# Grouping the value and score products of two units of a top-k attention + SwiGLU kernel, on one core

## The chip, the cores and the metric

The kernel runs on one core of one Trainium2 chip. The metric is the device time of one execution, in microseconds (us), as the median of several runs. Engine names are those of the profile: PE is the matrix engine (TensorE) with PEld for its weight loads, DVE the vector engine, ACT the scalar engine, POOL the GpSimd engine, SP the engine that issues most DMAs.

## The reference: what is computed

Attention over 8 batches, 8 heads, 576 positions and head dimension 64, in which every query keeps only its 32 largest scores, followed by a gated feed-forward network (FFN) over the 4608 resulting rows:

```python
B, H, S, D = 8, 8, 576, 64
scores = scale * np.matmul(q, k.transpose(0, 1, 3, 2))
kth = np.partition(scores, -32, axis=-1)[..., -32:-31]
scores = np.where(scores >= kth, scores, -1e9)
attn = np.exp(scores - scores.max(-1, keepdims=True))
attn = attn / (attn.sum(-1, keepdims=True) + 1e-9)
x = np.matmul(attn, v).transpose(0, 2, 1, 3).reshape(B * S, H * D)   # 4608 x 512
g = x @ w_gate                                                      # 512 -> 1536
out = (g / (1 + np.exp(-g)) * (x @ w_val)) @ w_out                  # 1536 -> 512
```

All data are float32.

## The kernel before

The work is cut into 160 **units**. A unit is one batch, one query tile and one pair of heads; a batch has 5 query tiles x 4 pairs = 20 units. Query tiles 0 to 3 hold 128 queries (a *full* unit, both heads side by side in 1152 columns); query tile 4 holds the last 64 queries of both heads, one head above the other in 128 partitions (a *last* unit, 576 columns). With S = 576, J = 4 and JP = 512, R = 64 is what is left over: the last keys of each head.

One pass of the main loop, called iteration n here, has a stage of several units in it, in a fixed program order per engine:

```python
TURN, VALUES = 3, 4
for n in range(NU + VALUES):
    topk = select(n)                      # DVE: 4 x MAX8, 3 x MATCH_REPLACE8 per head, then e
    nxt = scores(n + 1)                   # PE products, ACT copies out of PSUM
    ahead = fetch(n + 2)                  # prep of a head pair, loads
    ...
    flush(on_act)                         # ACT: pending evacuations of the FFN
    penalize(n - 1)                       # POOL: e = e + scores
    flush(on_pool)
    run(turn(n - TURN))                   # PE transposes of e, ACT copies
    finish_unit(n - VALUES)               # values(): PE, ACT copy to xT
    next(nxt, None)                       # PE products of the scores
    early[0]()
    weigh(n - 1)                          # ACT: exp with sums
    run(nxt)                              # ACT: copies of the scores
    dve(2, beside=False)
    ...
    pieces(2)                             # PE: FFN work, as much as `credit` allows
    flush(on_act)
    dve(1); dve(1)
    run(norm)                             # ACT: scale e of unit n-2
    flush(on_pool)
    next(ahead, None); pieces(1); next(ahead, None)
    dve(1); pieces(1); dve(2); run(topk); pieces(6)
```

The stages that the change touches. PSUM tiles tagged "t" rotate over five banks (`ps_t`, bufs=5), those of the FFN over three others (`ps_f`):

```python
def prep(i):                                   # one head pair of one batch
    slab = slabs.tile([P, R + S + S], FP32, tag="kqT", name="kqT")
    for n, at in ((0, R), (None, S), (1, S + 2 * R)):
        ps = ps_t.tile([P, 512], FP32, tag="t", name="kqps")
        if n is None:                          # last keys and queries
            nc.tensor.transpose(ps[:, 0:P], kq_last[:].rearrange("p h d -> p (h d)"), ident[:])
            nc.scalar.copy(slab[:, at : at + P], ps[:, 0:P])
            nc.scalar.copy(slab[:, 0:R], ps[:, 0:R])
            yield
            continue
        for c in range(J):                     # 4 transposes, then one copy
            ...

def scores(n):
    sc = work.tile([P, 2 * S], FP32, tag="sc", name="sc", bufs=2)
    half = S // 2                              # 288
    if qt == J:
        ...                                    # 4 products of 64x64 tiles, 288 columns
    else:
        for i in range(2):
            for hh, d in enumerate(halves):    # d: partitions 0-63 or 64-127
                ps = bank()
                nc.tensor.matmul(ps[:, 0:half], slab[d, q0 : q0 + P], slab[d, k0 : k0 + half])
        yield
        for i, ps in banks:
            nc.scalar.copy(sc[:, i * half : (i + 1) * half], ps[:, 0:half])

def turn(n):                                   # e^T, 9 (full) or 5 (last) transposes
    for c0, cn in ((0, J), (J, 1)) if last else ((0, J), (J, 1), (J + 1, J)):
        ps = ps_t.tile([P, 512], FP32, tag="t", name="etps")
        ...
        nc.scalar.copy(et[0:kl, c0 : c0 + cn, :], ...)

def values(n):
    av = ps_t.tile([P, P], FP32, tag="t", name="av")
    if not last:                               # last keys of both heads, block diagonal
        nc.tensor.matmul(av[:], vl[:], et[:, J, :], start=True, stop=False)
    for c in range(J + 1 if last else J):
        for hh in range(2):                    # column tiles of 64: one head each
            nc.tensor.matmul(av[hh * R : (hh + 1) * R, 0:ql],
                             v_last[:, hh, :] if c == J else vt[:, hh, c, :], moving, ...)
    ...                                        # ACT copies av into xT

def share(n):                                  # FFN pieces that iteration n may do
    others = 0.0
    for m, cost in ((n + 1, 0.7), (n - TURN, 0.6), (n - VALUES, 0.7)):
        if m >= 0:
            others += cost * (0.5 if units[m][1] == J else 1)
    if units[n + 2][1] == 0:
        others += 0.6
    beside = 6.4 if T[1] else 7.0
    return beside * n_heads(units[n][1]) / 2 - others
```

The FFN works on blocks of 256 rows. From the second block on, its output product is done by seven `quarter(...)` products with sums on POOL; a piece of the two input products is 16 PE records, a piece of a quarter 6 records (three products; every float32 product stands in the trace as two MATMUL records). `load(i)` fetches keys and queries of a head pair with six DMAs (`k` of two heads, last keys, `q` of two heads, last queries) into a pool of two buffers. At the end of the kernel every engine's instructions are tied to program order.

Of the kernel before, what the change touches and what calls it, by code (L numbers as in the profile page):

```python
# [1 line left out]

# [13 lines left out]
P = 128  # L16
# [4 lines left out]
BLK = 256  # L21
# [6 lines left out]
def kernel(  # L28
# [34 lines left out]

    nc = tc.nc
    B, H, S, D = q.shape
    DM, DFF = w_gate.shape
# [10 lines left out]
    assert D == 64 and R == 64 and H * D == DM and DM == 512 and B * S % BLK == 0  # L79

    consts = ctx.enter_context(tc.tile_pool(name="consts", bufs=1))
    ld = ctx.enter_context(tc.tile_pool(name="ld", bufs=2))
    slabs = ctx.enter_context(tc.tile_pool(name="slabs", bufs=4))
    work = ctx.enter_context(tc.tile_pool(name="work", bufs=2))
    small = ctx.enter_context(tc.tile_pool(name="small", bufs=3))
# [4 lines left out]

    ident = consts.tile([P, P], FP32, name="ident")
    make_identity(nc, ident[:])
    NV = 4
    vlast = []
    for i in range(NV):
        vt = consts.tile([P, P], FP32, name=f"vlast{i}")
        nc.vector.memset(vt[:], 0.0)
        vlast.append(vt)
# [120 lines left out]

    pairs = [(b, hp) for b in range(B) for hp in range(NHP)]  # L220
    raw, preps = {}, {}

    def load(i):
        b, hp = pairs[i]
        h = slice(2 * hp, 2 * hp + 2)
        kq = ld.tile([P, 2, J, 2, D], FP32, tag="kq", name="kq_in")
        kq_last = ld.tile([P, 2, D], FP32, tag="kql", name="kq_last")
        for n, src in ((0, k), (1, q)):
            for hh in range(2):
                queue = nc.scalar if hh == 1 and i == 0 else nc.sync  # L230
                queue.dma_start(
                    kq[:, n, :, hh, :],
                    src[b, 2 * hp + hh, 0:JP].rearrange("(p j) d -> p j d", j=J),
                )
            nc.sync.dma_start(
                kq_last[n * R : (n + 1) * R], src[b, h, JP:S].rearrange("h p d -> p h d")
            )
        raw[i] = (kq, kq_last)
# [3 lines left out]
    def load_v(i):  # L242
        b, hp = pairs[i]
        h = slice(2 * hp, 2 * hp + 2)
        vt = slabs.tile([P, 2, J, D], FP32, tag="v", name="v")
        v_last = slabs.tile([R, 2, D], FP32, tag="vl", name="v_last")
        vl = vlast[i % NV]
        nc.sync.dma_start(
            vt[:].rearrange("p h j d -> p h (j d)"),
            v[b, h, 0:JP].rearrange("h (p j) d -> p h (j d)", j=J),  # L250
        )
        nc.sync.dma_start(v_last[:], v[b, h, JP:S].rearrange("h p d -> p h d"))
        for hh in range(2):
            o = hh * R
            nc.sync.dma_start(vl[o : o + R, o : o + R], v[b, 2 * hp + hh, JP:S])
        vs[i] = (vt, v_last, vl)

    def prep(i):

        kq, kq_last = raw.pop(i)  # L260
        slab = slabs.tile([P, R + S + S], FP32, tag="kqT", name="kqT")
        for n, at in ((0, R), (None, S), (1, S + 2 * R)):
            ps = ps_t.tile([P, 512], FP32, tag="t", name="kqps")
            if n is None:
                nc.tensor.transpose(
                    ps[:, 0:P], kq_last[:].rearrange("p h d -> p (h d)"), ident[:]
                )
# [17 lines left out]

        return 1 if qt == J else 2

    def scores(n):
        b, qt, hp = units[n]
        slab = preps[b * NHP + hp]  # L290
        sc = work.tile([P, 2 * S], FP32, tag="sc", name="sc", bufs=2)
        halves = [slice(0, D), slice(D, P)]
        half = S // 2

        def bank():
            return ps_t.tile([P, 512], FP32, tag="t", name="s")


        if qt == J:
            banks = [bank() for _ in range(2)]  # L300
            for i, ps in enumerate(banks):
                for d in halves:
                    k0 = R + i * half
                    nc.tensor.matmul(  # L304
                        ps[d, 0:half], slab[d, S + R : S + 2 * R], slab[d, k0 : k0 + half]
                    )
            yield
            for i, ps in enumerate(banks):
                nc.scalar.copy(sc[:, i * half : (i + 1) * half], ps[:, 0:half])  # L309
        else:  # L310
            q0 = S + 2 * R + qt * P
            banks = []
            for i in range(2):
                for hh, d in enumerate(halves):
                    ps = bank()
                    banks.append((i + 2 * hh, ps))
                    k0 = (1 - hh) * R + i * half
                    nc.tensor.matmul(  # L318
                        ps[:, 0:half], slab[d, q0 : q0 + P], slab[d, k0 : k0 + half]
                    )  # L320
            yield
            for i, ps in banks:
                nc.scalar.copy(sc[:, i * half : (i + 1) * half], ps[:, 0:half])  # L323
        state[n] = dict(sc=sc)

    def select(n):

# [77 lines left out]

    xT, done = {}, {}

    def values(n):

        b, qt, hp = units[n]  # L410
        vt, v_last, vl = vs[b * NHP + hp]
        et = state.pop(n)["et"]
        last = qt == J
        ql = R if last else P
        av = ps_t.tile([P, P], FP32, tag="t", name="av")
        if not last:
            nc.tensor.matmul(av[:], vl[:], et[:, J, :], start=True, stop=False)  # L417
        for c in range(J + 1 if last else J):
            kl = R if c == J else P
            for hh in range(2):  # L420
                moving = (
                    et[0:kl, c, hh * R : (hh + 1) * R]
                    if last
                    else et[:, c + hh * (J + 1), :]
                )
                nc.tensor.matmul(  # L426
                    av[hh * R : (hh + 1) * R, 0:ql],
                    v_last[:, hh, :] if c == J else vt[:, hh, c, :],
                    moving,
                    start=last and c == 0,  # L430
                    stop=c == (J if last else J - 1),
                )
        c0 = b * S + qt * P
        at = c0
        while at < c0 + ql:
            kb = at // BLK
            n_c = min((kb + 1) * BLK, c0 + ql) - at
            if kb not in xT:
                xT[kb] = ffn.tile([P, NHP, BLK], FP32, tag="xT", name="xT", bufs=3)
                done[kb] = 0  # L440
            nc.scalar.copy(
                xT[kb][:, hp, at - kb * BLK : at - kb * BLK + n_c],
                av[:, at - c0 : at - c0 + n_c],
            )
            done[kb] += n_c
            at += n_c

    def store(o, g0):

# [220 lines left out]
    def fetch(n):  # L670
# [2 lines left out]
        i = b * NHP + hp  # L673
        if qt == 0:
            yield from prep(i)
        if qt == J and i + NHP < len(pairs):
            load(i + NHP)

    def share(n):


        others = 0.0
        for m, cost in ((n + 1, 0.7), (n - TURN, 0.6), (n - VALUES, 0.7)):
            if m >= 0:
                others += cost * (0.5 if units[m][1] == J else 1)
        if units[n + 2][1] == 0:
            others += 0.6

        beside = 6.4 if T[1] else 7.0
# [7 lines left out]
    def run(steps):  # L697
        for _ in steps:
            pass

    def finish_unit(n):
        values(n)
        b, qt, hp = units[n]
        if qt == J and b + 1 < B:
            load_v((b + 1) * NHP + hp)

    load(0)
    rounding(2)
    load(1)
    run(fetch(0))  # L710
    run(scores(0))
    run(fetch(1))
    credit = [0.0]
    no = iter(())
    over = {}
    TURN, VALUES = 3, 4
    due = [2.0]
    for n in range(NU + VALUES):
# [33 lines left out]
        run(nxt)  # L752

        dve(2, beside=False)
        if 2 <= n + 2 < NHP:
            load(n + 2)
# [9 lines left out]
        flush(on_pool)  # L766
        next(ahead, None)
        pieces(1)
        next(ahead, None)
        dve(1)  # L770
        pieces(1)
        dve(2)
# [52 lines left out]
```

## Time and profile before

| | before |
|---|---|
| median of 3 runs | 1840.44 us (1838.14 to 1840.71) |
| profiled execution, span | 1835.9 us |
| DVE busy | 1618.9 us (88%) |
| ACT busy | 1202.6 us (66%) |
| POOL busy | 1013.0 us (55%) |
| MAX8 on DVE, L339 | 1152 of about 758 ns |
| PE: FFN input products, L480 | 3456 records of 382 ns |
| PE: score products of full units, L318 | 1024 records, 64-row tiles, 288 columns, 445 ns |
| PE: value products, L426 | 2560 records |
| ACT: copies of 128x288 scores, L323 | 512 of 402 ns |
| ACT: copies of 128x512, L398 | 288 of 600 ns; 128x128: 128 of 278 ns |

How to read it: "busy" counts the modelled duration of an instruction. PE records overlap (a record of 382 ns starts every 216 ns in a run of equal ones), so what a stage costs on PE is read from the starts of its records, not from the durations. A chain of waits follows the work that ended last back to the start and says which engine the time was spent on.

### The profile page before, as it was taken

The page shows a single profiled execution, that of the slowest core. Times are in us where ns is not written, and L with a number is a line of the kernel's source. Part 1 is how long each engine was busy: PE and PEld are TensorE (multiplying, and loading weights), DVE is VectorE, ACT ScalarE, POOL GpSimd, SP SyncE. Part 2 cuts the span into 40 slices and gives each one's busy share as a digit, 9 for nine tenths or more (in the row PEclk, how much of TensorE's full clock was granted, in tenths as well). Part 3 has the DMA queues.
Part 4 walks back from the last instruction along what each step waited for, and adds up shares of the span by engine and source line. Part 5 has one row for each costly group of instructions (what it writes and reads, how often), then busy time and mean ns, then how long its engine had stood idle before and what let it go on. Part 6 is the DMA issues. An engine that isn't in the chain of part 4 may idle for free.

```text
span 1835.9 us, 30517 instructions
## 1 busy us (share of the span) xinstructions
PE 1705.2 (93%) x10756; PEld 1406.3 (77%) x10756; DVE 1618.9 (88%) x3405; ACT 1202.6 (66%) x2943; POOL 1013.0 (55%) x932
## 2 busy tenths in 40 slices
PE   3448999999999989999999999999999999999998
PEld 2336758777888878887888878888788878888887
DVE  7999999999999889997999989998999989998300
ACT  5667766677666667666767676767776766675431
POOL 3556746645555545655464646564556554646444
PEclk7668999999999999999999999999999999999999
DMA  7332121000200021000300012000300011000000
GB/s 189 98 84 91 59 66 26 12 1 21 73 1 12 2 66 27 12 1 15 73 19 1 12 42 52 1 12 2 74 19 12 1 36 32 1 12 12 1 13 12
DMA packets 109145, 59.65 MB, mean 32 GB/s; under 512 B 88512, under 2 KB 96704, under 8 KB 108992
## 3 DMA queue, kind: packets, MB, share of 16 engines
q1 hardware_dynamic: 107936, 57.44, 12.1%
q8 instruction: 85, 1.39, 0.3%
q14 instruction: 68, 0.56, 0.1%
q10 hardware_dynamic: 1056, 0.26, 0.1%
HBM read 48.23 MB, written 9.44 MB: 31 GB/s over the span
## 4 chain that ended last, share of the span: by engine, by line
PE 83%; DVE 3%; POOL 2%; ACT 2%; issue 2%; POOLq 0%; ACTq 0%
PE f L480 39%; PE x_ps L566 9%; PE av L426 8%; PE etps L397 7%; PE s L318 7%; PE y_ps L566 7%; PE s L304 2%; PE av L417 1%; DVE m L339 1%; PE kqps L273 1%; DVE rest L343 1%; PE o_ps L526 1%; POOL e L361 1%; POOL p L552 0%; ACT e L370 0%
## 5 line engine op out<-in xcount | busy, mean ns | idle before, releaser
L339 DVE MAX8 m<-rest 128x8 f32<-128x576 f32 x864 | 619.3, 758 | 2.2
L343 DVE MATCH_REPLACE8 rest<-m,rest 128x576 f32<-128x576 f32 x576 | 427.1, 754 | 0.0
L361 POOL TENSOR_TENSOR e<-e,sc 128x1152 f32<-128x1152 f32 (+1 forms) x160 | 382.7, 2392 | 79.7 <-DVE e L349 61.0
L480 PE MATMUL f<-xT,wg 128*128 128x256 f32 x1728 | 401.6, 382 | 0.0
L480 PE MATMUL f<-xT,wv 128*128 128x256 f32 x1728 | 400.4, 382 | 0.0
L480 PEld LDWEIGHTS f<-xT,wg 128*128 128x128 f32 x1728 | 323.0, 190 | 62.6 <-issue 21.0
L480 PEld LDWEIGHTS f<-xT,wv 128*128 128x128 f32 x1728 | 325.3, 190 | 59.5 <-issue 16.6
L508 POOL TENSOR_TENSOR h<-h,half_g 128x512 f32<-128x512 f32 x108 | 138.1, 1279 | 295.6 <-ACT h L507 295.1
L339 DVE MAX8 m<-sc 128x8 f32<-128x576 f32 x288 | 206.4, 757 | 105.8 <-ACT sc L309 57.9
L370 ACT ACTIVATE e<-e,bias 128x576 f32<-128x576 f32 x288 | 222.1, 777 | 89.5 <-POOL e L361 89.5
L397 PE MATMUL etps<-ident,e 128*128 128x128 f32 (+1 forms) x1312 | 184.0, 285 | 96.9 <-POOL size L120 40.8
L398 ACT COPY et<-etps 128x512 f32<-128x512 f32 (+1 forms) x448 | 184.4, 484 | 124.6 <-PE etps L397 123.6
L397 PEld LDWEIGHTS etps<-ident,e 128*128 128x128 f32 (+1 forms) x1312 | 158.3, 146 | 124.3 <-POOL size L120 43.3
L513 POOL TENSOR_TENSOR h<-h,val 128x512 f32<-128x512 f32 x108 | 139.9, 1295 | 186.0 <-ACT val L512 185.8
L385 ACT ACTIVATE e<-e,tot 128x576 f32<-128x576 f32 x288 | 211.9, 789 | 7.0 <-DVE tot L382 6.7
L343 DVE MATCH_REPLACE8 rest<-m,sc 128x576 f32<-128x576 f32 x288 | 213.0, 750 | 0.0
L318 PE MATMUL s<-kqT 64*128 64x288 f32 x1024 | 171.6, 445 | 5.8 <-ACT kqT L278 3.6
L349 DVE TENSOR_SCALAR e<-sc,m 128x576 f32<-128x576 f32 x288 | 171.8, 640 | 3.4
L426 PE MATMUL av<-et,v 128*64 128x128 f32 (+1 forms) x2560 | 172.4, 280 | 0.0
L323 ACT COPY sc<-s 128x288 f32<-128x288 f32 x512 | 163.9, 402 | 1.8 <-PE s L318 1.7
L426 PEld LDWEIGHTS av<-et,v 128*64 128x64 f32 x2560 | 135.7, 144 | 22.7 <-issue 6.6
L505 ACT ACTIVATE h<-f 128x512 f32<-128x512 f32 x108 | 65.3, 605 | 130.9 <-PE f L480 130.9
(71 smaller groups left out, 2010.0 us busy)
## 6 DMA issues: line engine op xcount, KB each, us to landing
v<-in_v_dram SPq DMA_DIRECT2D x32, 256.0 KB, 3.0
kq_in<-in_k_dram SPq DMA_DIRECT2D x63, 128.0 KB, 3.0
kq_in<-in_q_dram SPq DMA_DIRECT2D x63, 128.0 KB, 3.0
w<-in_moe_w_gate_dram SPq DMA_DIRECT2D x12, 512.0 KB, 3.7
w<-in_moe_w_val_dram SPq DMA_DIRECT2D x12, 512.0 KB, 3.8
w<-in_moe_w_out_dram SPq DMA_DIRECT2D x12, 512.0 KB, 3.6
out_dram<-o SPq DMA_DIRECT2D x40, 128.0 KB, 2.4
out_dram<-o SPq DMA_DIRECT2D x16, 256.0 KB, 2.4
```

Of the source, the lines that this page charges most:

```text
L318: nc.tensor.matmul(ps[:, 0:half], slab[d, q0 : q0 + P], slab[d, k0 : k0 + half])
L339: nc.vector.max(m[:, t, 8 * r : 8 * r + 8], cur[:, hs])
L343: nc.vector.match_replace(rest[:, hs], m[:, t, 8 * r : 8 * r + 8], cur[:, hs], LOWEST)
L349: nc.vector.tensor_scalar(e[:, hs], sc[:, hs], m[:, t, TOP_K - 1 : TOP_K], FAR, ALU.is_lt, ALU.mult)
L361: nc.gpsimd.tensor_tensor(e[:, every], e[:, every], sc[:, every], ALU.add)
L370: nc.scalar.activation(e[:, hs], e[:, hs], AF.Exp, bias=bias[:, t : t + 1], scale=scale, accum_out=tot[:, t : t + 1],)
L385: nc.scalar.mul(e[:, hs], e[:, hs], tot[:, t : t + 1])
L397: nc.tensor.transpose(ps[0:kl, c * P : (c + 1) * P], e[:, k0 : k0 + kl], ident[:])
L398: nc.scalar.copy(et[0:kl, c0 : c0 + cn, :], ps[0:kl, 0 : cn * P].rearrange("p (c j) -> p c j", c=cn),)
L426: nc.tensor.matmul(av[hh * R : (hh + 1) * R, 0:ql], v_last[:, hh, :] if c == J else vt[:, hh, c, :], moving, start=last and c == 0, stop=c ...
L480: nc.tensor.matmul(ps[:, i, :], w[:, kc, m * P : (m + 1) * P], x[:, kc, :], start=(kc == 0), stop=(kc == KC - 1),)
L566: nc.tensor.matmul(ps, lhsT, T[i][m], start=m == 0, stop=m == MQ - 1)
```

## The change

It does four things. It puts the value products of two units and the score products of two units next to each other, in odd iterations only, so that PE goes through its tile shapes (128x128, 128x64 for values, 64x128 for scores) once for two units. It computes the scores against the last keys of both heads as one 128x128 product with a block-diagonal `klast`, placed beside the like product with `vlast`, and the other 512 keys of a head in one product with 512 columns instead of two with 288. It has three score buffers, so that two units can be ahead, and finds the room by giving the loads one buffer (the first loads borrow buffers of the FFN). And it moves the transposes of odd iterations behind the first FFN pieces, fetches a head pair one iteration earlier, and has new constants for how much FFN work an iteration takes.

The diff, cut to its core:

```diff
-    ld = ctx.enter_context(tc.tile_pool(name="ld", bufs=2))
+    ld = ctx.enter_context(tc.tile_pool(name="ld", bufs=1))
+    klast, vlast = [], []                       # [P, P] each, zeroed, one per head pair
 ...
 def load(i):
+        if 1 <= i < NHP:
+            kq = ffn.tile([P, 2, J, 2, D], FP32, tag="xT", name="kq_in", bufs=3)
+            kq_last = ffn.tile([P, 4, 2, D], FP32, tag="h", ...)[:, 0]
+        else:
+            kq = ld.tile(...); kq_last = ld.tile(...)[:]
 ...
 def prep(i):
-        slab = slabs.tile([P, R + S + S], FP32, tag="kqT", name="kqT")
+        slab = slabs.tile([P, JP + S], FP32, tag="kqT", name="kqT")
-                nc.scalar.copy(slab[:, at : at + P], ps[:, 0:P])
-                nc.scalar.copy(slab[:, 0:R], ps[:, 0:R])
+                for d in HALVES:
+                    nc.scalar.copy(klast[pairs[i][1]][d, d], ps[d, 0:R])
+                nc.scalar.copy(slab[:, at : at + R], ps[:, R:P])
 ...
-    def scores(n):
+    def scores(ns):
+        scs = [work.tile([P, 2 * S], FP32, tag="sc", name="sc", bufs=3) for _ in ns]
+        last = bank("last")
+        for u, (slab, hp) in enumerate(of):
+            if qt < J:
+                nc.tensor.matmul(last[:, u * P : (u + 1) * P], slab[:, queries], klast[hp][:])
+        yield
+        for u, ((slab, hp), sc) in enumerate(zip(of, scs)):
+            if qt == J:
+                mains = [bank("s")]
+                for d in HALVES:
+                    nc.tensor.matmul(mains[0][d, :], slab[d, queries], slab[d, 0:JP])
+                for d in HALVES:
+                    nc.tensor.matmul(last[d, u * P : u * P + R], slab[d, queries], klast[hp][d, d])
+            else:
+                mains = [bank("s") for _ in HALVES]
+                for d, ps in zip(HALVES, mains):
+                    nc.tensor.matmul(ps[:], slab[d, queries], slab[d, 0:JP])
+            yield
+            for hh, ps in enumerate(mains):
+                nc.scalar.copy(sc[:, hh * (S + R) : hh * (S + R) + JP], ps[:])
+            ...                                  # and the unit's part of `last`
 ...
-    def values(n):
+    def values(ns, nxt):
+        avs = [ps_t.tile([P, P], FP32, tag="t", name="av") for _ in ns]
+        if not last:
+            for n, et, av in zip(ns, ets, avs):
+                nc.tensor.matmul(av[:], vl[:], et[:, J, :], start=True, stop=False)
+        next(nxt, None)                          # the products with klast
+        for n, et, av in zip(ns, ets, avs):
+            ...                                  # as before, unit after unit
 ...
 def fetch(n):
-        if qt == J and i + NHP < len(pairs):
-            load(i + NHP)
+            if NHP <= i + 1 < len(pairs):        # right after prep(i)
+                load(i + 1)
 ...
 def share(n):
-        others = 0.0
-        for m, cost in ((n + 1, 0.7), (n - TURN, 0.6), (n - VALUES, 0.7)):
-            if m >= 0:
-                others += cost * (0.5 if units[m][1] == J else 1)
+        others = 0.6
+        if n % 2 == 1:
+            for m in (n - 5, n - 4, n + 1, n + 2):
+                if m >= 0:
+                    others += 0.3 if units[m][1] == J else 0.6
 ...
+    load(2)                                      # beside load(0) and load(1), ahead of the loop
 ...                                              # main loop
-        nxt = scores(n + 1) if n + 1 < NU else no
-        ahead = fetch(n + 2) if n + 2 < NU else no
+            nxt = scores([n + 1, n + 2]) if n % 2 == 1 and n + 2 < NU else no
+            ahead = fetch(n + 3) if n + 3 < NU else no
 ...
-        if 0 <= n - TURN < NU:
+        if n % 2 == 0 and n >= TURN:
             run(turn(n - TURN))
-        if n >= VALUES:
-            finish_unit(n - VALUES)
-        next(nxt, None)
+        if n % 2 == 1 and n >= 5:
+            finish_units([n - 5, n - 4], nxt)
+        else:
+            next(nxt, None)
+        for _ in range(2):
+            next(nxt, None)                      # products of unit n+1; its copies, products of n+2
         early[0]()
         if 0 <= n - 1 < NU:
             weigh(n - 1)
         run(nxt)                                 # copies of unit n+2
 ...
         pieces(2)
         flush(on_act)
+        if n % 2 == 1 and 0 <= n - TURN < NU:
+            run(turn(n - TURN))
```

More of the change, by code (lines that the diff above doesn't have):

```diff
@@ L1 @@
 from contextlib import ExitStack
+from itertools import chain
 import concourse.bass as bass
@@ L92 @@
     make_identity(nc, ident[:])
[L93 to L98, printed above, removed]
+    klast, vlast = [], []
+    for i in range(NHP):
+        for name, tiles in (("klast", klast), ("vlast", vlast)):
+            t = consts.tile([P, P], FP32, name=f"{name}{i}")
+            nc.vector.memset(t[:], 0.0)
+            tiles.append(t)
     eps = consts.tile([P, 1], FP32, name="eps")
@@ L221 @@
     raw, preps = {}, {}
+    HALVES = [slice(0, D), slice(D, P)]
     def load(i):
@@ L225, in load @@
         h = slice(2 * hp, 2 * hp + 2)
-        kq = ld.tile([P, 2, J, 2, D], FP32, tag="kq", name="kq_in")
-        kq_last = ld.tile([P, 2, D], FP32, tag="kql", name="kq_last")
+        if 1 <= i < NHP:
+            kq = ffn.tile([P, 2, J, 2, D], FP32, tag="xT", name="kq_in", bufs=3)
+            kq_last = ffn.tile([P, 4, 2, D], FP32, tag="h", name="kq_last", bufs=MS + 1)[:, 0]
+        else:
+            kq = ld.tile([P, 2, J, 2, D], FP32, tag="kq", name="kq_in")
+            kq_last = ld.tile([P, 2, D], FP32, tag="kql", name="kq_last")[:]
         for n, src in ((0, k), (1, q)):
@@ L246, in load_v @@
         v_last = slabs.tile([R, 2, D], FP32, tag="vl", name="v_last")
-        vl = vlast[i % NV]
+        vl = vlast[hp]
         nc.sync.dma_start(
@@ L260, in prep @@
         kq, kq_last = raw.pop(i)
-        slab = slabs.tile([P, R + S + S], FP32, tag="kqT", name="kqT")
-        for n, at in ((0, R), (None, S), (1, S + 2 * R)):
+        slab = slabs.tile([P, JP + S], FP32, tag="kqT", name="kqT")
+        for n, at in ((0, 0), (None, JP), (1, S)):
             ps = ps_t.tile([P, 512], FP32, tag="t", name="kqps")
@@ L265, in prep @@
                 nc.tensor.transpose(
-                    ps[:, 0:P], kq_last[:].rearrange("p h d -> p (h d)"), ident[:]
+                    ps[:, 0:P], kq_last.rearrange("p h d -> p (h d)"), ident[:]
                 )
-                nc.scalar.copy(slab[:, at : at + P], ps[:, 0:P])
-                nc.scalar.copy(slab[:, 0:R], ps[:, 0:R])
+                for d in HALVES:
+                    nc.scalar.copy(klast[pairs[i][1]][d, d], ps[d, 0:R])
+                nc.scalar.copy(slab[:, at : at + R], ps[:, R:P])
                 yield
@@ L286, in n_heads, with bank @@
         return 1 if qt == J else 2
-    def scores(n):
[L289 to L303, printed above, removed]
+    def scores(ns):
+        scs = [work.tile([P, 2 * S], FP32, tag="sc", name="sc", bufs=3) for _ in ns]
+        for n, sc in zip(ns, scs):
+            state[n] = dict(sc=sc)
+        def bank(name):
+            return ps_t.tile([P, 512], FP32, tag="t", name=name)
+        qt = units[ns[0]][1]
+        wide = R if qt == J else P
+        at = JP if qt == J else S + qt * P
+        queries = slice(at, at + wide)
+        of = [(preps[units[n][0] * NHP + units[n][2]], units[n][2]) for n in ns]
+        last = bank("last")
+        for u, (slab, hp) in enumerate(of):
+            if qt < J:
+                nc.tensor.matmul(
+                    last[:, u * P : (u + 1) * P], slab[:, queries], klast[hp][:]
+                )
+        yield
[5 more added lines that the diff above has]
+                for d in HALVES:
@@ L304, in scores @@
                     nc.tensor.matmul(
-                        ps[d, 0:half], slab[d, S + R : S + 2 * R], slab[d, k0 : k0 + half]
+                        last[d, u * P : u * P + R], slab[d, queries], klast[hp][d, d]
                     )
+            else:
+                mains = [bank("s") for _ in HALVES]
+                for d, ps in zip(HALVES, mains):
+                    nc.tensor.matmul(ps[:], slab[d, queries], slab[d, 0:JP])
             yield
[L308 to L319, printed above, removed]
-                    )
-            yield
-            for i, ps in banks:
-                nc.scalar.copy(sc[:, i * half : (i + 1) * half], ps[:, 0:half])
@@ L324, in scores @@
-        state[n] = dict(sc=sc)
+            for hh, ps in enumerate(mains):
+                nc.scalar.copy(sc[:, hh * (S + R) : hh * (S + R) + JP], ps[:])
+            if qt < J or u == len(ns) - 1:
+                for v in (u,) if qt < J else range(len(ns)):
+                    nc.scalar.copy(
+                        scs[v][:, JP : JP + wide], last[:, v * P : v * P + wide]
+                    )
     def select(n):
@@ L406 @@
     xT, done = {}, {}
-    def values(n):
-        b, qt, hp = units[n]
-        vt, v_last, vl = vs[b * NHP + hp]
-        et = state.pop(n)["et"]
+    def values(ns, nxt):
+        b, qt, _ = units[ns[0]]
         last = qt == J
         ql = R if last else P
-        av = ps_t.tile([P, P], FP32, tag="t", name="av")
+        ets = [state.pop(n)["et"] for n in ns]
+        avs = [ps_t.tile([P, P], FP32, tag="t", name="av") for _ in ns]
         if not last:
[L417 to L424, printed above, removed]
-                )
[L426 to L446, printed above, removed]
@@ new lines, in values @@
+            for n, et, av in zip(ns, ets, avs):
+                vl = vs[b * NHP + units[n][2]][2]
+                nc.tensor.matmul(av[:], vl[:], et[:, J, :], start=True, stop=False)
+        next(nxt, None)
+        for n, et, av in zip(ns, ets, avs):
+            hp = units[n][2]
+            vt, v_last, _ = vs[b * NHP + hp]
+            for c in range(J + 1 if last else J):
+                kl = R if c == J else P
+                for hh in range(2):
+                    moving = (
+                        et[0:kl, c, hh * R : (hh + 1) * R]
+                        if last
+                        else et[:, c + hh * (J + 1), :]
+                    )
+                    nc.tensor.matmul(
+                        av[hh * R : (hh + 1) * R, 0:ql],
+                        v_last[:, hh, :] if c == J else vt[:, hh, c, :],
+                        moving,
+                        start=last and c == 0,
+                        stop=c == (J if last else J - 1),
+                    )
+            c0 = b * S + qt * P
+            at = c0
+            while at < c0 + ql:
+                kb = at // BLK
+                n_c = min((kb + 1) * BLK, c0 + ql) - at
+                if kb not in xT:
+                    xT[kb] = ffn.tile([P, NHP, BLK], FP32, tag="xT", name="xT", bufs=3)
+                    done[kb] = 0
+                nc.scalar.copy(
+                    xT[kb][:, hp, at - kb * BLK : at - kb * BLK + n_c],
+                    av[:, at - c0 : at - c0 + n_c],
+                )
+                done[kb] += n_c
+                at += n_c
@@ L675, in fetch @@
             yield from prep(i)
-        if qt == J and i + NHP < len(pairs):
-            load(i + NHP)
+            if NHP <= i + 1 < len(pairs):
+                load(i + 1)
     def share(n):
-        others = 0.0
-        for m, cost in ((n + 1, 0.7), (n - TURN, 0.6), (n - VALUES, 0.7)):
-            if m >= 0:
-                others += cost * (0.5 if units[m][1] == J else 1)
-        if units[n + 2][1] == 0:
+        others = 0.6
[3 more added lines that the diff above has]
+                    others += 0.3 if units[m][1] == J else 0.6
+        if units[n + 3][1] == 0:
             others += 0.6
@@ L699, in run, with finish_units @@
             pass
[L701 to L705, printed above, removed]
+    def finish_units(ns, nxt):
+        values(ns, nxt)
+        for n in ns:
+            b, qt, hp = units[n]
+            if qt == J and b + 1 < B:
+                load_v((b + 1) * NHP + hp)
     load(0)
@@ L709 @@
     load(1)
+    load(2)
     run(fetch(0))
-    run(scores(0))
+    run(scores([0]))
     run(fetch(1))
@@ L715 @@
     over = {}
-    TURN, VALUES = 3, 4
+    TURN = 3
     due = [2.0]
-    for n in range(NU + VALUES):
+    for n in range(NU + 4):
         nh = n_heads(units[n][1]) if n < NU else 1
@@ L721 @@
         over[n - 1] = normalize(n - 1) if 0 <= n - 1 < NU else no
-        nxt = scores(n + 1) if n + 1 < NU else no
-        ahead = fetch(n + 2) if n + 2 < NU else no
+        if n == 0:
+            nxt, ahead = scores([1]), chain(fetch(2), fetch(3))
+        else:
+            nxt = scores([n + 1, n + 2]) if n % 2 == 1 and n + 2 < NU else no
+            ahead = fetch(n + 3) if n + 3 < NU else no
         norm = over.pop(n - 2, no)
@@ L742 @@
         flush(on_pool)
-        if 0 <= n - TURN < NU:
+        if n % 2 == 0 and n >= TURN:
             run(turn(n - TURN))
-        if n >= VALUES:
-            finish_unit(n - VALUES)
-        next(nxt, None)
+        if n % 2 == 1 and n >= 5:
+            finish_units([n - 5, n - 4], nxt)
+        else:
+            next(nxt, None)
+        for _ in range(2):
+            next(nxt, None)
         early[0]()
@@ L754 @@
         dve(2, beside=False)
-        if 2 <= n + 2 < NHP:
-            load(n + 2)
+        if n == 0:
+            load(3)
         if n < NHP:
@@ L768 @@
         pieces(1)
-        next(ahead, None)
+        run(ahead)
         dve(1)
```

## The prediction

> **What bounds the kernel now.** I read the page's head and its chain of waits first, then busy time by stretches, then single starts on the timeline.
>
> ```profile
> PE 1705.2 (93%) x10756; PEld 1406.3 (77%) x10756; DVE 1618.9 (88%) x3405; ACT 1202.6 (66%) x2943; POOL 1013.0 (55%) x932
> ...
> PE   3448999999999989999999999999999999999998
> ...
> DVE  7999999999999889997999989998999989998300
> ...
> PE 83%; DVE 3%; POOL 2%; ACT 2%; issue 2%; POOLq 0%; ACTq 0%
> ```
>
> ```profile
> 100.00:150.00 50.00, 23.56 (x138) 18.65 (x137) 48.99 (x107) 32.83 (x76) 29.29 (x25) 0.67 0.32 86
> ...
> 1300.00:1400.00 100.00, 99.81 (x629) 83.81 (x626) 99.62 (x209) 66.31 (x166) 57.30 (x52) 1.00 0.15 36
> ...
> 1700.00:1750.00 50.00, 50.00 (x285) 42.79 (x284) 16.78 (x33) 22.78 (x50) 24.36 (x27) 1.00 0.00 1
> ```
>
> The columns of the second view are length, then busy us of PE, PEld, DVE, ACT and POOL. Until about 185 us DVE is full and PE half idle: nothing saved on PE counts there. From then on PE is full, and after about 1720 us it works alone on what is left of the FFN. DVE is nearly full in the middle, but each stretch of PE time that is freed there can take FFN work which otherwise stands at the end. So the time is PE's work after 185 us plus PE's waits, and I count only these.
>
> Next, what one visit to the value and score products costs:
>
> ```profile
> 1005.97 1.15 PE L397 MATMUL etps<-ident,e 128*128 128x128 f32 x9
> 1006.95 0.39 PE L417 MATMUL av<-et,vlast 128*128 128x128 f32 x2
> 1007.27 1.09 PE L426 MATMUL av<-et,v 128*64 128x128 f32 x16
> 1008.29 1.24 PE L318 MATMUL s<-kqT 64*128 64x288 f32 x8
> 1009.46 2.86 PE L566 MATMUL y_ps<-wo,h 128*128 128x256 f32 x12
> ```
>
> ```profile
> 1012.32 5.18 PE x_ps L566 x24
> ```
>
> This line is of the chain in order of time, those above of PE's timeline; the first number is the start. I use starts alone. Nine transposes take 0.98 us, 0.109 each; 24 records of 256 columns take 5.18, 0.216 each, or 0.84 ns a column. Narrower windows of the timeline show value and score records starting two at a time, in different tiles of the array, so 16 value records are 8 slots and 8 score records 4 slots. At these rates two `vlast` records are worth 0.22, the values 8 x 0.109 = 0.87, the scores 4 x 288 x 0.84 = 0.97. The starts give 0.32, 1.02 and 1.17, and the first FFN record is followed after 0.32 (1009.46, then 1009.78 in a narrow window) and not 0.216. The surplus, 0.10 + 0.15 + 0.20 + 0.10 = **0.55 us a visit**, sits where the tile shape changes, part before the first record of a shape and part behind it.
>
> **What the Trainium skill says.** "TensorEngine Tiling (Array Packing)", Key Properties, says that changing the tiling mode drains the engine. The trace agrees: about 0.1 us ahead of each new shape. "TensorE: Matmul & The Clock Gate", Part 2, says that weight loads are normally pulled ahead of running products; the other half of the surplus, behind the first record of a shape, is what I would expect where that could not be done, but no view names the cause. "ScalarE: Activation LUTs", What ACT_TABLE_LOAD costs, gives one element a cycle plus a fixed part. The trace has 402 ns for 288 columns and 600 ns for 512, so two wide copies are cheaper than four narrow ones.
>
> **The change part by part.**
>
> *Fewer visits.* Two units share one visit: minus 0.55 us for two full units.
>
> *More score work.* Before, 0.97 us a full unit. After, 2 records of 128 columns for the last keys, 0.22 at the transposes' rate, and 2 slots of 512 columns, 2 x 0.43 = 0.86: 1.08. Plus 0.11 a unit, 0.23 a pair. So an ordinary pair gains 0.55 - 0.23 = **0.32 us**. The block-diagonal product multiplies zeros, but it stands among products of the same shape and adds no switch.
>
> *Last units.* A batch has ten pairs. In six, both stages hold full units: 6 x 0.32. In two, the values are of last units and go through a second tile shape that returns for the second unit, so I count only 0.39 less 0.23 = 0.16. In two, the scores are of last units: 0.97 becomes 2 x 0.43 + 2 x 0.06 = 0.98, while the switches there, by their starts, are worth 0.45, so 0.43. Sum 1.9 + 0.3 + 0.9 = 3.1 us a batch, 25 us for eight, less the first 13 or so iterations where DVE is the bound (2 us): **23 us of PE work saved**.
>
> *ACT.* Four copies of 402 become two of 600 and one of 278: 130 ns less in a full unit, 17 us of 1203. ACT is at 66%; that is beside the path, except for the wait below.
>
> *FFN pacing.* By the constants a batch's iterations now allow 79.2 pieces where 76.8 were allowed; a batch needs 2.25 blocks x 34.5 = 77.6. That moves 2.4 x 1.73 = 4.2 us of PE work a batch from the end into the loop, which is where the saved 3.1 us go. It shortens the PE-only end and does not alter the sum.
>
> **The rivals.**
>
> *A wait for banks takes the place of the switches.* Thirteen PSUM tiles of two iterations rotate over five banks. In an odd iteration they are two `av`, `last`, four `s`, then the transposes: the first `etps` gets the bank of `last`, which is free only when ACT has copied the second unit's scores, behind `weigh`. Take the start of the first unit's scores as 0. PE has its banks full at about 1.15. ACT copies the first unit until 2.3, then needs for `weigh` what it needs here:
>
> ```profile
> 1008.57 0.78 ACT L370 ACTIVATE e<-e,bias 128x576 f32<-128x576 f32 x1
> 1009.25 0.19 ACT L370 ACTIVATION_READ_ACCUMULATOR e<-e,bias 128x1 f32 x1
> ...
> 1010.43 1.28 ACT L323 COPY sc<-s 128x288 f32<-128x288 f32 x4
> ```
>
> From 1008.57 to 1010.43 are 1.86 us, so 4.15, and the second unit's copies end at about 5.4. PE ends the scores at 1.9, pays 0.1, and has two FFN pieces before the transposes: 2 x 1.73 brings it to 5.5, no wait; two pieces of the output quarters, 2 x 1.30, only to 4.6, a wait of 0.8. Quarters are 10.5 of 34.5 cost units of a block, 30%. Over some 70 odd iterations: 70 x 0.3 x 0.8 = 17 us.
>
> *A late load.* With one buffer the next pair's load starts when the last transposes of the pair before it are done. One load is six issues of some 0.63 us:
>
> ```profile
> 1082.99 0.62 SPq L235 DMA_DIRECT2D kq_last<-in_k_dram  x1
> 1083.71 1.25 SPq L231 DMA_DIRECT2D kq_in<-in_k_dram  x2
> 1085.01 1.29 SPq L231 DMA_DIRECT2D kq_in<-in_q_dram  x2
> 1086.35 0.63 SPq L235 DMA_DIRECT2D kq_last<-in_q_dram  x1
> ```
>
> From the first issue to the start of the sixth are 3.4 us, plus the 2.4 that the page gives for the landing of `kq_last`: 5.8. The preps fall into the short iterations of last units, some 5.5 to 7 us. PE then has about 4.5 us of other work in two of three cases a batch, waiting perhaps 1 and 1.5 us: up to 2.5 a batch, 17 us, of which some 2 a batch are waits that PE has there now. Net 7 us.
>
> *Waits that go.* Waits of PE between 200 and 1720 us add up to some 30 us, half of them around last units, the longest 4.6 at 650, where turns wait for ACT and DVE for scores. A third score buffer lets DVE run further ahead. I take 8 us off.
>
> *DVE becomes the bound.* It is busy for 1619 us and idle in the PE-only end. Its waits for score copies (58 + 48 us) should shrink; with 1619 plus 10 at the start plus one FFN block of about 60 at the end its floor is near 1700. I rule this out.
>
> **The range and the chances.** 1840 - 23 + 15 (of the 24 that the two new waits could cost) - 8 = **1824 us**. With neither new wait, and old waits gone, about 1800; with both in full and no old wait gone, 1841, and with POOL late for `weigh` in many iterations some more: **1799 to 1847**. Over 2% faster means under 1803.6: 0.13. Over 2% slower, above 1877, needs a wait I have not seen: 0.05. Within 2%: 0.82.
>
> **What would show it.** In the timeline of PE after, an odd iteration should have 4 `vlast` and 4 `klast` records, 32 of V, 8 of scores with 512 columns a full pair, about 4.9 us from the first to the second FFN record, where two visits now take 2 x 2.62. Idle time of PE ahead of `etps` released by ACT's score copies shows the first rival; idle ahead of `kqps` released by a DMA the second. DVE's waits for score copies should fall. The prediction is wrong if grouped products do not keep their slots (512-column records not starting in pairs), if the transposes wait in ordinary iterations as well, or if the end without DVE grows.

## The result and the profile after

The changed kernel takes 1862.67 us (median of 4 runs, 1860.86 to 1863.32) against 1840.58 for the kernel before on the same chip: **1.2% slower**, ratio 1.0121 with a 95% interval of 1.0103 to 1.0138. The prediction was 1824, with 1799 to 1847 as its range.

The head of the page and its chain of waits, for the changed kernel:

```profile
PE 1703.5 (92%) x10500; PEld 1386.7 (75%) x10500; DVE 1639.4 (88%) x3409; ACT 1198.9 (64%) x2847; POOL 1013.5 (54%) x932
...
PE 70%; ACT 10%; POOL 4%; DVE 2%; issue 1%; DMA 0%; POOLq 0%; SPq 0%; ACTq 0%; DVEq 0%
```

PE's busy time has hardly moved. What moved is the chain: the part on PE falls from 83% to 70%, and ACT, 2% before, has 10%. The chain that ends last now runs more often through results of other engines that PE waits for.

A visit for two units, on PE's timeline (start, length, engine, line, operation, tiles, shape, count):

```profile
1018.46 0.61 PE L439 MATMUL av<-et,vlast 128*128 128x128 f32 x4
1018.91 0.61 PE L318 MATMUL last<-klast,kqT 128*128 128x128 f32 x4
1019.45 1.97 PE L452 MATMUL av<-et,v 128*64 128x128 f32 x32
1021.35 1.99 PE L334 MATMUL s<-kqT 64*128 64x512 f32 x8
1023.26 2.86 PE L592 MATMUL x_ps<-wo,h 128*128 128x256 f32 x12
```

From 1018.46 to 1023.26 are 4.80 us for two units. Before it was 2.51 for one (1006.95 to 1009.46), 5.02 for two, and the 0.10 behind the first FFN record was paid twice. So an ordinary pair saves 0.33 us. By medians of all visits after 185 us, pairs whose scores are of last units take 4.53 against 2 x 2.46, 0.49 saved with the 0.10. Pairs whose values are of last units save nothing: with the `klast` products at their head they take 4.21 (1141.61 to 1145.82 in one of them) against 2 x 2.05. With 42, 16 and 14 such visits the grouping is worth **22 us of PE time**. It is not in the result because of this (waits of PE after 185 us: who, for whom, us in total, times, longest). The kernel before:

```profile
PE etps L397 <- issue: 15.3, 9, 3.5
PE etps L397 <- ACT e L385: 10.9, 8, 4.6
PE kqps L265 <- ACT sc L323: 2.5, 2, 1.6
```

The changed kernel:

```profile
PE etps L415 <- ACT e L403: 12.2, 12, 3.2
PE kqps L286 <- ACT sc L337: 9.8, 9, 1.3
PE etps L415 <- ACT sc L337: 8.9, 4, 3.1
PE s L334 <- ACT xT L467: 7.8, 6, 1.7
PE x_ps L592 <- POOL h L640: 6.2, 6, 1.7
PE etps L415 <- issue: 3.6, 5, 0.7
...
PE kqps L286 <- DMA kq_in<-in_q_dram: 1.5, 1, 1.5
```

The first view adds up to 31 us with its small rows, the second to 59. There is more of everything and no single new wait: scaled e (`ACT e L403`), score copies, copies of values, sums on POOL. Beyond the idle time that these rows name, the starts of transposes and preps lie 21 us further apart in total than their rates, against 10 before. Most of this is waiting too: idle time counts from the modelled end of a record, 0.27 us behind its start for a transpose, so a short wait does not appear in the rows and a long one appears too short. A stretch at a batch boundary shows it:

```profile
1087.80 2.00 PE L506 MATMUL f<-xT,wg 128*128 128x256 f32 x8
1089.63 1.15 PE L415 MATMUL etps<-ident,e 128*128 128x128 f32 x9
...
1091.96 0.66 PE L286 MATMUL kqps<-ident,kq_in 128*128 128x128 f32 x4 [0.64 <-ACT et L416]
1093.33 1.75 PE L415 MATMUL etps<-ident,e 128*128 128x128 f32 x9 [0.72 <-POOL bias L377]
1094.92 3.62 PE L506 MATMUL f<-xT,wv 128*128 128x256 f32 x16
```

The nine transposes at 1089.63 are over in 0.98; those at 1093.33, which come with nothing in between but a prep, take 1.59. Two more waits are inside: the fifth starts at 1093.95, 0.05 us after ACT has scaled its part of e, the sixth at 1094.43, 0.05 us after a copy of ACT. One FFN piece (1.73 us) is all that stands between the scores, which end at 1087.8, and two sets of transposes. (A piece of the input products is 8 records, four products, and not the 16 records given above.)

The whole balance, from start to start over all of PE's records after 185 us: idle time between records grows by 30 us, transposes take 8 us more and preps 4 more; the visits, those held up inside included, take 18 less, the FFN as long as before. That makes 24 us, the difference of the spans.

### The profile page after: what moved, and what is told of

It reads as the page before. It is cut to its first block, busy times and chain, and to the rows that moved or that the text cites. A ratio compares the mean times of both kernels' runs of the same rounds, so it can differ in the third digit from the quotient of the medians.

```text
span 1860.2 us, 29955 instructions
## 1 busy us (share of the span) xinstructions
PE 1703.5 (92%) x10500; PEld 1386.7 (75%) x10500; DVE 1639.4 (88%) x3409; ACT 1198.9 (64%) x2847; POOL 1013.5 (54%) x932
## 4 chain that ended last, share of the span: by engine, by line
PE 70%; ACT 10%; POOL 4%; DVE 2%; issue 1%; DMA 0%; POOLq 0%; SPq 0%; ACTq 0%; DVEq 0%
PE f L506 36%; PE x_ps L592 7%; PE av L452 7%; PE etps L415 5%; PE s L334 5%; PE y_ps L592 4%; ACT e L388 2%; ACT et L416 2%; ACT e L403 2%; ACT sc L337 1%; PE s L326 1%; PE last L318 1%; DVE m L357 1%; PE av L439 1%; DVE rest L361 1%; POOL e L379 1%
## 5 line engine op out<-in xcount | busy, mean ns | idle before, releaser
L415 PE MATMUL etps<-ident,e 128*128 128x128 f32 (+1 forms) x1312 | 190.8, 287 | 71.5 <-ACT sc L337 45.5
L403 ACT ACTIVATE e<-e,tot 128x576 f32<-128x576 f32 x288 | 211.5, 787 | 12.3 <-DVE tot L400 12.3
L367 DVE TENSOR_SCALAR e<-sc,m 128x576 f32<-128x576 f32 x288 | 188.5, 691 | 3.4
L337 ACT COPY sc<-s 128x512 f32<-128x512 f32 x288 | 154.7, 583 | 54.8 <-PE s L334 44.5
L334 PE MATMUL s<-kqT 64*128 64x512 f32 x512 | 141.5, 652 | 43.5 <-ACT xT L467 36.8
L467 ACT COPY xT<-av 128x128 f32<-128x128 f32 (+1 forms) x192 | 41.3, 241 | 181.8 <-PE av L452 181.7
L452 PE MATMUL av<-et,v 128*64 128x128 f32 (+1 forms) x2560 | 152.2, 271 | 0.0
```

Of the source, the lines that this page charges most:

```text
L334: nc.tensor.matmul(ps[:], slab[d, queries], slab[d, 0:JP])
L367: nc.vector.tensor_scalar(e[:, hs], sc[:, hs], m[:, t, TOP_K - 1 : TOP_K], FAR, ALU.is_lt, ALU.mult)
L403: nc.scalar.mul(e[:, hs], e[:, hs], tot[:, t : t + 1])
L415: nc.tensor.transpose(ps[0:kl, c * P : (c + 1) * P], e[:, k0 : k0 + kl], ident[:])
L452: nc.tensor.matmul(av[hh * R : (hh + 1) * R, 0:ql], v_last[:, hh, :] if c == J else vt[:, hh, c, :], moving, start=last and c == 0, stop=c ...
```

## Experiments

Times are medians; each ratio is to the kernel before, run beside it.

| kernel | us | ratio (95% interval) |
|---|---|---|
| changed | 1862.7 | 1.0121 (1.0103 to 1.0138) |
| changed, banks 6 + 2 | 1861.9 | 1.0123 (1.0108 to 1.0138) |
| before, banks 6 + 2 | 1835.4 | 0.9979 (0.9969 to 0.9989) |
| changed, copies first | 1870.9 | 1.0173 (1.0157 to 1.0188) |
| changed, transposes later | 1852.4 | 1.0073 (1.0055 to 1.0090) |
| changed, even allowance | 1844.0 | 1.0025 (1.0017 to 1.0033) |
| changed, even + later | 1838.0 | 0.9992 (0.9985 to 0.9999) |
| changed, end | 1853.4 | 1.0075 (1.0060 to 1.0090) |
| changed, all three | 1830.8 | 0.9948 (0.9931 to 0.9965) |
| the same, load later | 1829.2 | 0.9940 (0.9925 to 0.9955) |
| before, wide scores | 1869.5 | 1.0163 (1.0146 to 1.0180) |
| before, wide, beside `vlast` | 1861.2 | 1.0119 (1.0103 to 1.0136) |
| before, uneven allowance | 1862.5 | 1.0129 (1.0114 to 1.0144) |
| before, end | 1839.7 | 1.0001 (0.9992 to 1.0009) |

**Is it the five banks?** My first theory was the prediction's first rival. Two runs change the number of banks in both kernels:

```diff
-    ps_t = ... bufs=5        ps_f = ... bufs=3
+    ps_t = ... bufs=6        ps_f = ... bufs=2
```

> The changed kernel with six banks for the attention's PSUM tiles and two for the FFN's. Bank theory (the loss is PE waiting for one of five rotating banks that ACT frees late): the waits of transposes, preps and scores for ACT's copies fall from some 28 us after 185 us to under 10, and the time falls by 10 to 20 us to 1843 to 1853, unless the FFN with two banks loses as much. Rival (the loss is the larger score product, the single load buffer or the FFN's pacing): these waits stay or move, time within 4 us of 1863 or above it.

> The control: the kernel before with six banks for attention and two for the FFN. It had few bank waits (2.5 us of preps waiting for score copies), so six banks can't gain much; what it loses is the price of two FFN banks alone, 0 to 15 us: 1838 to 1855. That price is to be taken off the run of the changed kernel with the same banks.

Two FFN banks cost the kernel before nothing (it gains 0.2%), and six attention banks give the changed kernel nothing on balance. Its waits after 185 us are 56 us against 59. Those of transposes and preps for score copies fall from 18.7 to 7.4 us; but transposes now wait 19.4 us for scaled e where they waited 12.2, and 6 us of waits for the two FFN banks are new, so a gain of up to 6 us may be hidden, not one of 10 to 20. The next run frees the bank of `last` earlier by putting the second unit's copies ahead of `weigh`:

```diff
-        weigh(n - 1)
         run(nxt)
+        weigh(n - 1)
```

> The changed kernel, but ACT copies the second unit's scores before weigh and not behind it. Bank theory: the bank of the last keys comes free 1.9 us earlier, the transposes' and preps' waits for score copies (19 us after 185 us) go to below 5 and the time falls by 10 to 20 us, to 1843 to 1853. Rival: exp comes later and delays the turn of that unit instead, or the waits were not what set the end: within 4 us of 1863.

It is 8 us slower. The waits for score copies all but vanish, and another takes their place. Two rows of its waits of PE:

```profile
PE etps L415 <- ACT e L403: 24.7, 15, 3.7
...
PE etps L415 <- ACT sc L337: 1.6, 2, 1.2
```

**The bank theory falls** as the main cause. In both runs the waits for score copies shrink and waits for e grow in their place; in the second exp also comes later, so that run alone would not decide.

**Is it uncovered latency?** Two runs leave the work of every stage as it is and put more FFN work between a result and its use. The first moves the odd iteration's transposes behind one more piece:

```diff
         pieces(2)
         flush(on_act)
-        if n % 2 == 1: run(turn(n - TURN))
         ...
         next(ahead, None)
         pieces(1)
+        if n % 2 == 1: run(turn(n - TURN))
         run(ahead)
```

> The changed kernel with the odd iteration's transposes one FFN piece later, behind the scaling of e. Bank theory: the transposes find their banks free, their waits for score copies (9 us) vanish, time falls by 5 to 12 us; the preps in front of which they stood keep theirs. Rival (waits move to whoever comes next): within 4 us of 1863.

10 us are gained, though the row for score copies that I had named doesn't vanish (14.3 us from 8.9); it is the waits for e that shrink, from 12.2 to 4.5. In all, the rows still add up to 58 us, so the expected size came out and the expected reason is not shown by this run alone. The second spreads the allowance of a pair of iterations evenly:

```diff
-        if n % 2 == 1:
-            for m in (n - 5, n - 4, n + 1, n + 2): others += 0.6     # 0.3 for a last unit
+        odd = n if n % 2 == 1 else n - 1
+        for m in (odd - 5, odd - 4, odd + 1, odd + 2): others += 0.3 # 0.15
```

> The changed kernel with the same FFN allowance a pair of iterations, but spread evenly over odd and even ones (before: 3.4 and 5.8 pieces; in odd iterations of last units nothing). Theory now, as six banks did not help: PE stands because the odd iterations leave it too little FFN work to cover the latency through ACT. Then its waits (55 us between 190 and 1740 us) fall by a third and the time by 8 to 20 us, to 1843 to 1855. Rival (the waits come from the order of the attention stages alone): within 4 us of 1863.

> Even FFN allowance and the odd iteration's transposes one piece later, together. Covered-latency theory: the two add up, as both put FFN work between a result and its use: 1832 to 1845. Rival: both take away the same waits, so no better than the 1852 of the later transposes alone.

The even allowance alone gives back 19 us of the 22, and the rows of waits fall from 59 to 48 us. Both together bring the kernel to the time of the one before. They add up only in part (19 and 10 make 25).

**Is it the grouping that needs this, or the pacing by itself?** The control puts the unevenness into the kernel before, with nothing else changed:

```diff
+        others += 1.2 if n % 2 == 1 else -1.2
```

> The kernel before with the changed kernel's unevenness of the FFN allowance alone: 1.2 pieces less in odd iterations, 1.2 more in even ones. If uneven pacing costs by itself, PE's waits grow from 29 us and the time by 5 to 20 us: 1846 to 1860. Rival (in this kernel each iteration holds its own values, scores and transposes, so the odd ones still have work to cover the waits): within 4 us of 1840.

It costs 23.4 us, as much as the whole change. Its waits of PE after 185 us are 45 us where they were 31, most of it in rows that were there before and one new one; transposes and preps lie 8 us further apart besides:

```profile
PE etps L397 <- issue: 18.3, 11, 3.6
PE etps L397 <- ACT e L385: 16.2, 16, 2.8
PE etps L397 <- POOL e L361: 6.2, 3, 2.4
```

The FFN's records after 185 us are as many as before, and from DVE's last unit to the end are 102 us, before 98: the work was not moved to the end. So pacing is a cost by itself. My rival, that each iteration of this kernel has work of its own to cover waits, is refuted.

**The end.** In the changed kernel the last FFN block but one is used up at iteration 159, and the last can't start before the values of iteration 163. Its timeline there:

```profile
1784.56 1.29 PE L415 MATMUL etps<-ident,e 128*128 128x128 f32 x5 [3.21 <-ACT e L403]
1787.15 1.33 PE L415 MATMUL etps<-ident,e 128*128 128x128 f32 x5 [1.29 <-ACT e L403]
```

From 1784.6 the granted clock is 0.5 for 10.2 us. The mend is to hold work back:

```diff
         if n >= NU - NHP:
-            credit[0] = 8.0
+            credit[0] = 5.0
```

> The changed kernel, but the last iterations may take 5 FFN pieces each and not 8, so that the last block but one lasts until the last values. The end theory: PE's waits of 4.7 us near 1785 and the halved clock behind them (10 us at 0.5) go, and the time falls by 5 to 9 us. Rival: the last block just ends later by what was held back: within 3 us of 1863.

> The kernel before with 5 FFN pieces an iteration at the end in place of 8. Its end has only 1 us of waits on PE (6 to 9 us with the halved clock in the changed kernel), so it should gain little: 1837 to 1841. If it gains as the changed kernel did (9 us), the lead of the mended version is mostly this.

> The changed kernel with all three mends: even FFN allowance, later transposes in odd iterations, 5 pieces an iteration at the end. If PE's uncovered waits are what turned the gain into a loss, the visits' saving (29 us by the traces: 42, 16 and 14 visits at 0.33, 0.49 and 0.53 us) should now show in part: 5 to 9 us under the 1838 of the two mends, 1828 to 1834, which is below the kernel before. Rival (the end was already covered by the even allowance): 1836 to 1840.

9 us gained in the changed kernel, none in the one before. With all three mends it takes 1830.8 us, half a per cent less than the kernel before. (The 29 us of the last expectation count 0.53 us for visits with values of last units, without their `klast` products; with them the saving is 22.) The lead is not all the grouping's: six banks alone bring the kernel before to 0.9979, and it was not run with later transposes.

**The start.** DVE ends its first unit at 29.6 us instead of 26.4. In the last mended version the third pair's load is moved into the first iteration:

```diff
     load(1)
-    load(2)
     ...
         if n == 0:
+            load(2)
             load(3)
```

> The same with the third head pair's load issued in the first iteration and not ahead of the loop, so that the second piece of weights comes sooner. DVE's first result lay 3.2 us later after the change, 1.3 of it from the wider first score product; if the other 1.9 are the load's place, the time falls by 1 to 3 us. Rival: DVE's early iterations are full in either case and the order of loads does not matter: within 1 us of the run before it in this list.

1.5 us less in the median, but the intervals overlap, and in its trace DVE's first unit ends at 30.9, not sooner; in the traces of the changed kernel with an unchanged start it ends anywhere from 29.6 to 31.9. The reason given for this run is wrong and its gain not established.

**What the wide score products cost.** One part of the change alone, in the kernel before:

```diff
-        4 x matmul(ps[:, 0:288], slab[d, q0 : q0 + P], slab[d, k0 : k0 + 288])
+        matmul(last[:, 0:P], slab[:, queries], klast[hp][:])
+        2 x matmul(ps[:], slab[d, queries], slab[d, 0:JP])
```

> One part of the change alone: the kernel before with the new score products (one 128x128 product with klast and one of 512 columns a head), unit by unit, with two score buffers and two load buffers. If PE's work sets the time, the 0.11 us a unit of the working costs 12 to 14 us and the wider first product 1 us at the start: 1850 to 1856. Rival: fewer PSUM tiles a unit (7 instead of 8) and 130 ns less ACT pay for it: 1837 to 1844.

It costs 30 us, twice what I expected. Its timeline says why:

```profile
1026.14 1.09 PE L419 MATMUL av<-et,v 128*64 128x128 f32 x16
1027.17 0.49 PE L309 MATMUL last<-klast,kqT 128*128 128x128 f32 x2
1027.59 1.13 PE L312 MATMUL s<-kqT 64*128 64x512 f32 x4
```

The full product stands between the 128x64 and the 64x128 tiles: two records take 0.42 us to the next start, not 0.22. I had forgotten this third shape when I wrote the expectation. The next run puts it beside `vlast`, as the change does.

> The kernel before with the wide score products unit by unit, as in the run that took 1869.5, but the product with klast right behind the one with vlast, where the tile shape is already 128x128. If 0.14 us of the 0.25 us a unit there were an extra change of tile shape, some 13 to 17 us come back and 12 to 16 stay: 1852 to 1857. Rival (the wide products themselves are slower than their slots): 1865 to 1870.

The median visit is 2.82 us in the first of the two and 2.62 in the second, against 2.51: in place it costs the predicted 0.11, out of place 0.31. The time comes back by 8 us, less than expected: the early product now waits 7.8 us for the copies of the prep (`last` for `kqT`). Grouped or not, these products are not free, and the grouping has to pay for them.

**A cheaper form of the last keys?** Two runs replace the product with zeros by two of 64-row tiles:

```diff
-        matmul(last[:, u * P : (u + 1) * P], slab[:, queries], klast[hp][:])
+        for d, ps in zip(HALVES, lasts):
+            matmul(ps[:, u * R : (u + 1) * R], slab[d, queries], klast[hp][d, d])
```

> The same again, with the last keys of a full unit as two products of 64-row tiles with 64 columns, in two banks, and no 128x128 product of zeros: 2 slots of 0.057 us in place of 0.22, so 0.11 us less PE work a unit. If PE's work sets the time: 9 to 13 us faster than the run before it, 1815 to 1823. Rival: a fourteenth PSUM tile in two iterations and a longer wait for the copies eat it up: within 4 us of it or slower.

> The same with six banks for attention and two for the FFN. If the extra tile of the 64-row form waits for a bank, this is 2 to 8 us faster than the run before it; if, as the first try of six banks said, banks are not what PE waits for, within 3 us of it.

They take 1858.2 and 1855.0 us (ratios 1.0095, 1.0080 to 1.0110, and 1.0077, 1.0062 to 1.0092), 29 and 26 us more than without it. The reason is on PE, in the first of the two:

```profile
1024.82 1.13 PE L330 MATMUL s<-kqT 64*128 64x512 f32 x4
1025.78 0.33 PE L332 MATMUL last<-klast,kqT 64*128 64x64 f32 x4
1025.95 1.79 PE L330 MATMUL s<-kqT 64*128 64x512 f32 x4
1027.22 0.69 PE L332 MATMUL last<-klast,kqT 64*128 64x64 f32 x4
```

The first unit runs in pairs (0.96 us for four wide records with the 0.10 behind the first). The second takes 1.27 for four, and its short products 0.62 where the first took 0.17. The median visit is 5.45 us and not 4.80. The second unit waits for ACT, which these lines do not show as idle time:

```profile
1025.98 1.07 ACT L337 COPY sc<-s 128x512 f32<-128x512 f32 x2 [0.78 <-PE s L330]
```

The first of these two copies ends at 1026.57, and the second unit's second wide product starts at 1026.62; the short products start at 1027.22, 0.05 us after ACT's copy of the first unit's part of `last`, which is in the same bank. With six banks the wide products keep step, and the wait for the copy of `last` remains:

```profile
972.02 1.08 PE L330 MATMUL s<-kqT 64*128 64x512 f32 x4
973.29 0.55 PE L332 MATMUL last<-klast,kqT 64*128 64x64 f32 x4 [0.19 <-ACT sc L340]
```

Its median visit is 5.31 us. So the rival named in the expectation is what happened. In the form with one `klast` product all products into `last` stand ahead of the copies out of it.

## Why the prediction was wrong

- **The saved work: right.** 23 us predicted, 22 measured by medians. The ordinary pair was 0.32 in the working and is 0.33; the pairs whose scores are of last units save 0.49 where 0.43 stood, those whose values are of last units nothing where 0.16 stood. The cost of the wide products, 0.11 a unit, is confirmed by the run with the product beside `vlast`. ACT's busy time fell by 4 us and not by 17, beside the path.
- **FFN pacing: the step that failed.** "It shortens the PE-only end and does not alter the sum" holds only if PE has no waits. I counted the pieces of a batch and not where they stand. In the changed kernel they are 5.8 in one iteration and 3.4 in the next, and none in the odd ones of last units. The same swing of 1.2 pieces up and down costs 23 us in the kernel before, with no grouping at all, and without it the changed kernel is 19 us faster. The end did not get shorter either: from DVE's last unit to the end are 103 us, before 98.
- **The wait for banks: seen, but not its cause, and its size by luck.** Transposes and preps wait 19 us for score copies, near the 17 predicted. But the 17 were for transposes in some 20 iterations; these wait 8.9 us in four places, and the preps, which I hadn't reckoned, the rest. Freeing the banks brought nothing on balance, so this term can't be added up by itself; what counts is how much work covers the whole way through ACT.
- **The late load: no.** The two rows of waits on loads after 185 us are 1.5 and 0.7 us, against 7.
- **Waits that go: no.** I took 8 us off. The transposes' waits for scaled e stayed (10.9 and 12.2). With a third score buffer DVE's waits for score copies did fall, from 106 to 87 us, but PE's are for ACT.
- **DVE as the bound: rightly ruled out.** It is at 88% in both kernels. That DVE starts 3.2 us later was not in the working.

The sum had -23, +15 and -8. Measured, it is -18 for all visits, those held up inside included, and +42 for waits: 30 as idle time and 12 between the starts of transposes and preps. The mended version agrees with a real saving: with the waits reduced (40 us after 185 us, from 59) it is 10 us faster than the kernel before.

What stays open: how uneven pacing turns into these waits is argued from their rows, not shown step by step. Only one uneven spread was run in each kernel, so that an even one is the best is not shown. The mended version keeps 9 us more of waits than the kernel before.

## What to carry to other kernels

Where one engine is full and fills its waits with work from another stage, that work is not a sum to be moved at will: count it per iteration, beside the latency it has to cover, and try an even spread first. When stages are grouped, spread the filler anew before you judge the grouping. A wait named in a profile may be only the first in a queue; take it away in one run and see whether another comes up, before building on it.

## What the runs showed of the hardware

In these traces a change of tile shape on PE cost about 0.1 us ahead of it and 0.05 to 0.10 behind it, and a full product out of place 0.20 us a visit (2.82 and 2.62). Products in two row tiles started 0.007 us apart. Pairs of 64-column products between pairs of 512-column ones did not break that step, neither in the last units of the changed kernel nor in the six-bank run above. Where it broke, with five banks, the second 512-column product started 0.05 us after the end of a copy by ACT, 0.67 us behind the first (1025.95 and 1026.62).
